# Attention backward loop: keys outermost, one-bank score tiles, own dP tiles, and dQ products in bursts that share a bank with the scores

## The chip, the cores and the metric

The kernel runs on one NeuronCore of a Trainium2 chip. The metric is the device time of one execution in microseconds (us), the median of several runs. All runs quoted here ran on one core, and all are counted as fast: none is more than 1.5% above the fastest run of its kernel. "Granted clock" is the share of its full clock that TensorE was given, as the profile records it.

A *unit* below is 128 queries by 512 keys for a group of four heads. The loop that is changed has 512 units: 8 head groups x 4 query blocks x 4 key blocks x 4 query tiles. A unit takes 20 matmuls, each placed in a quarter of TensorE's array: four scores, four dP, four K products (dK), four V products (dV), four dQ products. Scores and dP contract over 32 rows, so that up to four of them run side by side in different row groups; the others have 16 or 32 output columns and run four side by side in different column groups. I call four such matmuls a *group*.

## The reference, cut to what matters

The reference is a transformer block (layer norm with conditioning, 32-head attention with head size 16, a squared-ReLU MLP; 2048 tokens, width 512) and its gradients for all inputs. The loop in question computes the gradient of this part:

```python
scores = jnp.einsum('bhqd,bhkd->bhqk', q, k) * Dh ** (-0.5)
p = _softmax(scores, axis=-1)
o = jnp.einsum('bhqk,bhkd->bhqd', p, v)
```

For each unit it recomputes E = exp(scores) and forms dP and dS = dP x E. It sums dV from E and dK from dS over the queries. It sums dQ from the transpose of dS over the keys.

## The kernel before

```python
psu = ... tile_pool(name="psIu", bufs=3, space=PSUM)   # three tiles of two banks: scores AND dP
psa = ... tile_pool(name="psIa", bufs=1, space=PSUM)   # accVK and dqacc, a bank each
units = [(hg, qc, kc, qi) for hg in range(HG) for qc in range(QC) for kc in range(QC) for qi in range(4)]

def score_pair(u, pair):                       # two scores, one exp of 128x1024
    psS = psu.tile([P, 2, 512], F32, name="psS_u", tag="pu")
    for hi in range(2):
        r = 32 * (2 * pair + hi)
        PE.matmul(psS[:, hi, :], st["q"][r:r + 32, ...], st["k"][r:r + 32, ...], tile_position=(r, 0), ...)
    ACT.activation(E_u[:, 2 * pair:2 * pair + 2, :], psS[:], AF.Exp, scale=SCALE)

def dp_pair(u, pair):                          # two dP, one multiply of 128x1024
    psD = psu.tile([P, 2, 512], F32, name="psD_u", tag="pu")
    ...
    DVE.tensor_tensor(dS_u[:, 2 * pair:2 * pair + 2, :], psD[:], E_u[...], ALU.mult)

def transpose_unit(u):                         # dS to dS^T by DMA, 512 KB a unit
    SP.dma_start(out=dqt[hg, qc, kc][:, qi], in_=bst[u][1].rearrange("p h k -> p (h k)"), transpose=True)

def kv_quads(u):     # 4 K and 4 V products into accVK; evicted every 4 units, added up by POOL
    ...
def dq_quad(b, kt):  # 4 dQ products into dqacc; evicted every 16 units
    ...

for j in range(2 * NU + 18):                   # two steps a unit
    u = j // 2
    ...
    score_pair(u, j % 2)
    dp_pair((j - 1) // 2, (j - 1) % 2)
    if (j - 1) % 2 == 1: transpose_unit((j - 1) // 2)
    if j % 2 == 0: kv_quads(u - 2)
    v = u - 8
    if j % 2 == 1: dq_quad(block of v, v % 4)  # one dQ group in every unit
```

TensorE, ScalarE and VectorE run this in exactly the written order.

Of the kernel before, what the change touches and what calls it, by code (L numbers as in the profile page):

```python
# [14 lines left out]
AF = mybir.ActivationFunctionType  # L15
ALU = mybir.AluOpType
AX = mybir.AxisListType
BF = dt.bfloat16
F32 = dt.float32

P = 128
# [4 lines left out]
HG = 8  # L26
FF = 1792
FC = 14
SCALE = 0.25
# [5 lines left out]
def kernel(  # L35
# [6 lines left out]
    n = A_x.shape[1]  # L42
    assert A_x.shape[2] == D and n % 512 == 0 and n <= 2048
    TT = n // P
    QC = n // 512
# [7 lines left out]
    PE = nc.tensor  # L53
    DVE = nc.vector
    ACT = nc.scalar
    POOL = nc.gpsimd
    SP = nc.sync
# [50 lines left out]
    dQtP = dram.tile([HG, P, n], BF, name="dQtP")  # L108
    dVKtP = dram.tile([HG, P, n], BF, name="dVKtP")

    with ExitStack() as ph:
        wk = ph.enter_context(tc.tile_pool(name="prepA", bufs=1))
# [20 lines left out]
        for j in range(6):  # L133
            pm = psA.tile([P, 512], F32, name="pm", tag="pm")
            for ic in range(DC):
                PE.matmul(pm[:], sbcT[:, ic, :], wmod_nat[:, ic, j * 512:(j + 1) * 512],
                          start=(ic == 0), stop=(ic == DC - 1))
# [5 lines left out]
        for jb in range(24):  # L143
            for ic in range(DC):
                PE.matmul(pcol[:, jb:jb + 1], wmod_nat[:, ic, jb * P:(jb + 1) * P], siluc_colbf[:, ic:ic + 1],
                          start=(ic == 0), stop=(ic == DC - 1))
# [21 lines left out]
    for ic in range(DC):  # L168
        for t in range(3):
            src = wqkv_nat[:, ic, t * 512:(t + 1) * 512].rearrange("p (hg h d) -> p hg h d", hg=HG, h=4)  # L170
            dst = wpadT[:, ic, t].rearrange("p hg (h c) -> p hg h c", h=4)[:, :, :, 0:DH]
# [524 lines left out]
        POOL.memset(qz[i][:], 0.0)  # L696


    with ExitStack() as ph:
        strm = ph.enter_context(tc.tile_pool(name="phIs", bufs=2))  # L700
        ework = ph.enter_context(tc.tile_pool(name="phIe", bufs=3))
        tpool = ph.enter_context(tc.tile_pool(name="phIt", bufs=3))
        stg = ph.enter_context(tc.tile_pool(name="phIg", bufs=2))
        wk = ph.enter_context(tc.tile_pool(name="phIw", bufs=2))
        psu = ph.enter_context(tc.tile_pool(name="psIu", bufs=3, space=bass.MemoryType.PSUM))
        psa = ph.enter_context(tc.tile_pool(name="psIa", bufs=1, space=bass.MemoryType.PSUM))
        units = [(hg, qc, kc, qi) for hg in range(HG) for qc in range(QC) for kc in range(QC) for qi in range(4)]
        hst, bst, dqt = {}, {}, {}

        def load_head(hg):  # L710
            st = {}
            for key, src in (("q", QtP), ("k", KtP), ("v", VtP), ("do", dOtP)):
                st[key] = strm.tile([P, n], BF, name=f"i{key}", tag=f"i{key}")
                SP.dma_start(out=st[key][:], in_=src[hg])
            st["qz"] = qz[hg % 2]
            qs = strm.tile([P, TT, 64], BF, name="iqs", tag="iqs")
            ACT.dma_start(out=qs[:], in_=q_st[:, :, hg * 64:(hg + 1) * 64])
            POOL.tensor_scalar(qz[hg % 2][:, :, :, DH:2 * DH], qs.rearrange("p t (h d) -> p t h d", h=4),
                               SCALE, None, ALU.mult)
            st["acc"] = stg.tile([P, n], F32, name="dVKacc", tag="dVKacc", bufs=1)  # L720
            st["dq"] = stg.tile([P, n], BF, name="dQst", tag="dQst")
            hst[hg] = st

        def score_pair(u, pair):
            hg, qc, kc, qi = units[u]
            st = hst[hg]
            qt = qc * 4 + qi
            if pair == 0:
                bst[u] = (ework.tile([P, 4, 512], BF, name="E_u", tag="E_u", bufs=4),
                          ework.tile([P, 4, 512], BF, name="dS_u", tag="dS_u", bufs=4))  # L730
            E_u, dS_u = bst[u]
            psS = psu.tile([P, 2, 512], F32, name="psS_u", tag="pu")
            for hi in range(2):
                r = 32 * (2 * pair + hi)
                PE.matmul(psS[:, hi, :], st["q"][r:r + 32, qt * P:(qt + 1) * P], st["k"][r:r + 32, kc * 512:kc * 512 + 512],  # L735
                          start=True, stop=True, tile_position=(r, 0))
            ACT.activation(E_u[:, 2 * pair:2 * pair + 2, :], psS[:], AF.Exp, scale=SCALE)  # L737

        def dp_pair(u, pair):
            hg, qc, kc, qi = units[u]  # L740
            st = hst[hg]
            qt = qc * 4 + qi
            E_u, dS_u = bst[u]
            psD = psu.tile([P, 2, 512], F32, name="psD_u", tag="pu")
            for hi in range(2):
                r = 32 * (2 * pair + hi)
                PE.matmul(psD[:, hi, :], st["do"][r:r + 32, qt * P:(qt + 1) * P], st["v"][r:r + 32, kc * 512:kc * 512 + 512],  # L747
                          start=True, stop=True, tile_position=(r, 0))
            DVE.tensor_tensor(dS_u[:, 2 * pair:2 * pair + 2, :], psD[:], E_u[:, 2 * pair:2 * pair + 2, :], ALU.mult)  # L749

        def transpose_unit(u):
            hg, qc, kc, qi = units[u]
            if qi == 0:
                dqt[hg, qc, kc] = tpool.tile([P, 4, 16, P], BF, name="dsT", tag="dsT")
            SP.dma_start(out=dqt[hg, qc, kc][:, qi],
                         in_=bst[u][1].rearrange("p h k -> p (h k)"), transpose=True)

        cur = {}

        def kv_quads(u):  # L760
            hg, qc, kc, qi = units[u]
            st = hst[hg]
            qt = qc * 4 + qi
            E_u, dS_u = bst.pop(u)
            if qi == 0:
                cur["vk"] = psa.tile([P, 512], F32, name="accVK", tag="accVK")
            acc = cur["vk"]
            for hq in range(4):
                PE.matmul(acc[32 * hq:32 * hq + 32, :], st["qz"][:, qt, hq, :], dS_u[:, hq, :],  # L769
                          start=(qi == 0), stop=False, tile_position=(0, 32 * hq), skip_group_check=True)  # L770
            for hq in range(4):
                PE.matmul(acc[32 * hq:32 * hq + DH, :], dOs_tok[:, qt, (hg * 4 + hq) * DH:(hg * 4 + hq + 1) * DH], E_u[:, hq, :],  # L772
                          start=False, stop=(qi == 3), tile_position=(0, 32 * hq), skip_group_check=True)
            if qi == 3:
                dst = st["acc"][:, kc * 512:(kc + 1) * 512]
                if qc == 0:
                    ACT.activation(dst, acc[:], AF.Identity)
                else:
                    tmp = wk.tile([P, 512], F32, name="vktmp", tag="vktmp")
                    ACT.activation(tmp[:], acc[:], AF.Identity)  # L780
                    POOL.tensor_tensor(dst, dst, tmp[:], ALU.add)  # L781
                if qc == QC - 1 and kc == QC - 1:
                    vkb = stg.tile([P, n], BF, name="vkb", tag="vkb", bufs=1)
                    POOL.tensor_copy(vkb[:], st["acc"][:])
                    SP.dma_start(out=dVKtP[hg], in_=vkb[:])

        def dq_quad(b, kt):
            hg, qc, kc = b
            if kc == 0 and kt == 0:
                cur["dq"] = psa.tile([P, 512], F32, name="dqacc", tag="dqacc")  # L790
            acc = cur["dq"]
            tT = dqt[b]
            for hq in range(4):
                h = hg * 4 + hq
                PE.matmul(acc[32 * hq:32 * hq + 32, :], KS_tok[:, kc * 4 + kt, h * DH:h * DH + 32], tT[:, :, hq * 4 + kt, :],  # L795
                          start=(kc == 0 and kt == 0), stop=(kc == QC - 1 and kt == 3),
                          tile_position=(0, 32 * hq), skip_group_check=True)
            if kt == 3:
                del dqt[b]
                if kc == QC - 1:  # L800
                    ACT.activation(hst[hg]["dq"][:, qc * 512:(qc + 1) * 512], acc[:], AF.Identity)
                    if qc == QC - 1:
                        SP.dma_start(out=dQtP[hg], in_=hst[hg]["dq"][:])

        NU = len(units)
        load_head(0)
        with tc.manual_schedule(engines={PE.engine, ACT.engine, DVE.engine}):
            for j in range(2 * NU + 18):
                u = j // 2
                if j < 2 * NU:  # L810
                    if j % 2 == 0 and units[u][1:] == (0, 2, 0) and units[u][0] + 1 < HG:
                        load_head(units[u][0] + 1)
                    score_pair(u, j % 2)
                if 1 <= j <= 2 * NU:
                    dp_pair((j - 1) // 2, (j - 1) % 2)
                    if (j - 1) % 2 == 1:
                        transpose_unit((j - 1) // 2)
                if j % 2 == 0 and 2 <= u < NU + 2:
                    kv_quads(u - 2)
                v = u - 8  # L820
                if j % 2 == 1 and 0 <= v < NU:
                    hg, qc, kc, qi = units[v]
                    dq_quad((hg, qc, kc), qi)

    qpool.release()

# [202 lines left out]
```

## Time and profile before

| | before |
|---|---|
| time, median | 4181.09 us |
| the loop, first exp to last dQ product | 2214 to 3878 us: 1664 us, 3.25 us a unit |
| in 2300 to 3500 us: TensorE / VectorE / ScalarE busy | 99% / 76% / 68% |
| granted clock there | 0.51 |

Here is the table of windows of the kernel before, for 1200 us inside the loop. Its columns are the stretch, its length, each engine's busy time with the number of instructions, the granted clock, the DMA share and the GB/s.

```profile
core 0: us, PE busy (x) PEld busy (x) DVE busy (x) ACT busy (x) POOL busy (x), PEclk, DMA share, GB/s
2300.00:3500.00 1200.00, 1184.05 (x7420) 207.43 (x7419) 907.53 (x742) 813.84 (x858) 116.39 (x82) 0.51 0.97 180
```

TensorE is without a gap, but at half its clock. VectorE's instructions in the loop are all multiplies, two a unit, so 742 of them are 371 units, or 1200 / 371 = 3.23 us each.

The chain of waits of the kernel before, over one unit (start, length, what):

```profile
2902.89 0.61 PE psD_u L747 x2
2903.50 0.55 PE accVK L769 x4
2904.05 0.43 PE accVK L772 x4
2904.47 0.54 PE psS_u L735 x2
2905.01 0.01 PE psD_u L747 x2
2905.02 0.55 PE dqacc L795 x4
2905.57 0.54 PE psS_u L735 x2
2906.11 0.03 issue
```

These are six phases. In one (at 2904.47) scores and dP run together, and the second costs 0.01 us more. In the other pair they run apart: the scores at 2905.57 (they open the next unit), then the dP at 2906.13, which had to wait for an exp to free one of the three shared tiles.

The clock is 0.50 in almost the whole loop, and 1.00 once, for some 20 us. These are four windows of the kernel before: two ordinary ones, the one just ahead of the rise, and one within the full-clock stretch.

```profile
2500.00:2503.40 3.40, 3.37 (x24) 0.56 (x20) 2.61 (x3) 2.74 (x4) 0.25 (x1) 0.50 0.85 159
2510.00:2513.40 3.40, 3.38 (x22) 0.59 (x23) 2.61 (x3) 2.21 (x3) 0.00 (x0) 0.50 0.82 154
...
3070.40:3073.80 3.40, 3.40 (x26) 0.71 (x24) 2.46 (x3) 2.70 (x4) 0.34 (x1) 0.50 1.38 213
...
3085.00:3090.00 5.00, 4.47 (x42) 1.44 (x40) 4.56 (x4) 4.28 (x5) 0.00 (x0) 1.00 1.49 198
```

TensorE is 99 to 100% busy in the first three.

### The profile page before, as it was taken

What the parts mean: (1) busy time and instruction counts of PE and PEld (TensorE: products, weight loads), DVE (VectorE), ACT (ScalarE), POOL (GpSimd) and SP (SyncE); (2) the same over time, 40 slices, a digit from 0 to 9 for tenths busy, and PEclk for the clock granted to TensorE, in tenths of its full rate; (3) what the DMA queues carried; (4) which work ended last, traced back from release to release, by engine and by line L of the source; (5) the groups of instructions that cost most, each with busy time, mean ns of one, the idle gap of its engine ahead of it and who ended that gap; (6) DMA issues with size and microseconds to landing.
All of it is one profiled execution on the core that took longest, in us unless ns stands there. A gap on an engine that the chain in (4) does not pass through costs nothing.

```text
span 4177.6 us, 48252 instructions
## 1 busy us (share of the span) xinstructions
PE 3479.6 (83%) x18427; PEld 840.9 (20%) x18501; DVE 2070.4 (50%) x3136; ACT 2149.3 (51%) x2462; POOL 294.1 (7%) x314
## 2 busy tenths in 40 slices
PE   3689999999986935766558999999999999999656
PEld 1221111111122311322221111111111111111222
DVE  7640000000038724630056777777777777777582
ACT  0039999999960000000005666666666666666211
POOL 2000000000000000000140000000000000100000
PEclk7975555555557967965875555555555555555777
DMA  3120000000012342466547998999999999999313
GB/s 117 63 111 16 15 6 16 15 16 15 6 65 94 139 110 97 98 210 178 172 151 141 162 195 162 196 163 196 162 200 163 196 163 194 162 172 162 120 48 99
DMA packets 1230133, 497.73 MB, mean 119 GB/s; under 512 B 1162051, under 2 KB 1192263, under 8 KB 1228109
## 3 DMA queue, kind: packets, MB, share of 16 engines
q1 hardware_dynamic: 1207246, 464.23, 50.8%
q0 software_dynamic: 6144, 28.32, 2.3%
q10 hardware_dynamic: 16512, 2.10, 0.4%
q8 instruction: 145, 2.38, 0.2%
q14 instruction: 86, 0.70, 0.1%
HBM read 126.45 MB, written 82.47 MB: 50 GB/s over the span
## 4 chain that ended last, share of the span: by engine, by line
PE 41%; DMA 4%; DVE 3%; issue 3%; ACT 1%; SPq 1%; POOL 0%; ACTq 0%; DVEq 0%; POOLq 0%
PE psS_u L735 13%; PE psD_u L747 7%; PE accVK L769 7%; PE dqacc L795 7%; PE accVK L772 5%; SPq L956 1%; DVE dqkv_tok L860 1%; DMA stld<-stok_st 1%; DVE dh1acc L868 1%; DMA out_dram<-w2blk 0%; ACT E_u L737 0%; DMA iqs<-q_st 0%; POOL dOs_tokpad L620 0%; DMA xst_31079<-dQtP 0%; DMA dsT<-dS_u 0%
## 5 line engine op out<-in xcount | busy, mean ns | idle before, releaser
L749 DVE TENSOR_TENSOR dS_u<-psD_u,E_u 128x1024 bf16<-128x1024 f32 x1024 | 1253.3, 1225 | 451.6 <-PE psD_u L747 384.3
L737 ACT ACTIVATE E_u<-psS_u 128x1024 bf16<-128x1024 f32 x1024 | 1046.8, 1024 | 456.4 <-PE psD_u L747 414.0
L311 ACT ACTIVATE ET<-psST 128x1024 bf16<-128x1024 f32 x1024 | 938.8, 1770 | 0.0
L308 PE MATMUL psST<-qt_sb,kt_sb 32*128 32x512 bf16 x2048 | 622.5, 597 | 79.7 <-DMA kt_sb<-KtP 8.9
L747 PE MATMUL psD_u<-iv,ido 32*128 32x512 bf16 x2048 | 618.1, 594 | 18.6 <-ACT E_u L737 5.3
L735 PE MATMUL psS_u<-ik,iq 32*128 32x512 bf16 x2048 | 615.1, 599 | 12.0 <-DVE dS_u L749 5.4
L326 DVE COPY ostage<-oacc 128x512 f32<-128x512 f32 x32 | 22.1, 692 | 914.4 <-PE oacc L322 799.8
L772 PE MATMUL accVK<-E_u,dOs_tok 128*16 128x512 bf16 x2048 | 329.0, 631 | 0.0
L322 PE MATMUL oacc<-ET,vaug 128*32 128x512 bf16 x2048 | 317.0, 609 | 0.6 <-ACT ET L311 0.6
L795 PE MATMUL dqacc<-dsT,KS_tok 128*32 128x512 bf16 x2048 | 314.1, 604 | 3.3 <-DMA dsT<-dS_u 3.3
L595 ACT ACTIVATE w1blk<-aw_0_12805 128x512 bf16<-128x512 f32 x1 | 0.6, 597 | 554.5 <-PE aw_0_12805 L591 554.5
L735 PEld LDWEIGHTS <-iq 32*128 32x128 bf16 x2048 | 106.7, 99 | 664.8 <-issue 664.5
L308 PEld LDWEIGHTS <-kt_sb 32*128 32x128 bf16 x2048 | 105.4, 99 | 556.7 <-issue 556.7
L781 POOL TENSOR_TENSOR dVKacc<-dVKacc,vktmp 128x512 f32<-128x512 f32 x96 | 121.3, 1264 | 1341.6 <-ACT vktmp L780 1341.6
L747 PEld LDWEIGHTS <-ido 32*128 32x128 bf16 x2048 | 156.4, 100 | 275.2 <-issue 274.4
L769 PE MATMUL accVK<-dS_u,qz_14372 128*32 128x512 bf16 x1024 | 158.8, 608 | 0.0
L769 PE MATMUL accVK<-dS_u,qz_14371 128*32 128x512 bf16 x1024 | 157.0, 602 | 0.0
L515 PE MATMUL pds<-gfT,w2T 128*128 128x512 bf16 x219 | 55.5, 406 | 107.8 <-DVE dzT L518 79.1
L264 PE MATMUL ppad<-xn1T,wpadT 128*128 128x512 bf16 x376 | 96.6, 402 | 21.6 <-DVE stagep L267 16.2
L322 PEld LDWEIGHTS <-vaug 128*32 128x32 bf16 x2048 | 57.7, 102 | 224.1 <-issue 224.1
L795 PEld LDWEIGHTS <-KS_tok 128*32 128x32 bf16 x2048 | 57.8, 101 | 222.3 <-issue 222.0
L328 POOL CAST obf<-ostage 128x512 bf16<-128x512 f32 x32 | 19.6, 614 | 1059.1 <-DVE ostage L326 1059.1
(1251 smaller groups left out, 2776.6 us busy)
## 6 DMA issues: line engine op xcount, KB each, us to landing
dzld<-dztok_st POOLq DMA_DIRECT2D x32, 448.0 KB, 3.7
dzld<-dztok_st SPq DMA_DIRECT2D x32, 448.0 KB, 3.4
dsT<-dS_u SPq DMA_TRANSPOSE x512, 4.3
rT_st<-rT SPq DMA_DIRECT2D x4, 1792.0 KB
rtok_st<-rtok SPq DMA_DIRECT2D x16, 448.0 KB, 2.5
stok_st<-stok SPq DMA_DIRECT2D x16, 448.0 KB
rTb<-rT_st SPq DMA_DIRECT2D x4, 1792.0 KB
rtokb<-rtok_st SPq DMA_DIRECT2D x16, 448.0 KB, 11.7
```

Of the source, the lines that this page charges most:

```text
L264: PE.matmul(pp[:], wpadT[:, ic, which, hg, :], h1T[:, ic, qc * 512:(qc + 1) * 512], start=(ic == 0), stop=(ic == DC - 1))
L308: PE.matmul(ps[:, hi, :], kt_sb[r:r + 32, kt * P:(kt + 1) * P], qt_sb[r:r + 32, qc * 512:(qc + 1) * 512], start=True, stop=True, tile_posi ...
L311: ACT.activation(ET[:, 2 * pair:2 * pair + 2, :], ps[:], AF.Exp, scale=SCALE)
L322: PE.matmul(oacc[32 * hq:32 * hq + 32, :], lhsT, ET[:, hq, :], start=(kt == 0), stop=(kt == TT - 1), tile_position=(0, 32 * hq), skip_grou ...
L735: PE.matmul(psS[:, hi, :], st["q"][r:r + 32, qt * P:(qt + 1) * P], st["k"][r:r + 32, kc * 512:kc * 512 + 512], start=True, stop=True, tile ...
L737: ACT.activation(E_u[:, 2 * pair:2 * pair + 2, :], psS[:], AF.Exp, scale=SCALE)
L747: PE.matmul(psD[:, hi, :], st["do"][r:r + 32, qt * P:(qt + 1) * P], st["v"][r:r + 32, kc * 512:kc * 512 + 512], start=True, stop=True, til ...
L749: DVE.tensor_tensor(dS_u[:, 2 * pair:2 * pair + 2, :], psD[:], E_u[:, 2 * pair:2 * pair + 2, :], ALU.mult)
L769: PE.matmul(acc[32 * hq:32 * hq + 32, :], st["qz"][:, qt, hq, :], dS_u[:, hq, :], start=(qi == 0), stop=False, tile_position=(0, 32 * hq), ...
L772: PE.matmul(acc[32 * hq:32 * hq + DH, :], dOs_tok[:, qt, (hg * 4 + hq) * DH:(hg * 4 + hq + 1) * DH], E_u[:, hq, :], start=False, stop=(qi ...
L781: POOL.tensor_tensor(dst, dst, tmp[:], ALU.add)
L795: PE.matmul(acc[32 * hq:32 * hq + 32, :], KS_tok[:, kc * 4 + kt, h * DH:h * DH + 32], tT[:, :, hq * 4 + kt, :], start=(kc == 0 and kt == 0 ...
```

## The change

Its intent is to give scores and dP PSUM tiles of their own, so that they always overlap. PSUM has eight banks, and before, all were taken. With keys outermost the sum for V and K stays in PSUM for 16 units, and dQ becomes a sum of four groups that is evicted and added up by POOL. So dQ needs its bank only while its four groups run; these are done in a burst in two of every eight steps, and in the other six the bank serves as a third score bank.

```diff
-        psu = ... bufs=3      # 3 x 2 banks, scores and dP
-        psa = ... bufs=1      # accVK, dqacc
-        units = [(hg, qc, kc, qi) for hg ... for qc ... for kc ... for qi in range(4)]
+        psd = ... bufs=2      # 2 x 2 banks, dP
+        pss = ... bufs=2      # 2 x 1 bank, scores
+        psx = ... bufs=1      # accVK; "px": scores or dqacc
+        units = [(hg, kc, qc, qi) for hg ... for kc ... for qc ... for qi in range(4)]
...
+            if shared:
+                psS = psx.tile([P, 512], F32, name="psS_x", tag="px")
+            else:
+                psS = pss.tile([P, 512], F32, name="psS_u", tag="ps")
+            PE.matmul(psS[:], ...)                                       # one score
+            ACT.activation(bst[u][0][:, hq, :], psS[:], AF.Exp, scale=SCALE)   # one exp of 128x512
-            psD = psu.tile([P, 2, 512], F32, name="psD_u", tag="pu")
+            psD = psd.tile([P, 2, 512], F32, name="psD_u", tag="pd")
...  # accVK: evicted once in 16 units, straight to bf16; dqacc: evicted every 4 units, POOL adds
-                if j % 2 == 0 and 2 <= u < NU + 2:
-                    kv_quads(u - 2)
-                v = u - 8
-                if j % 2 == 1 and 0 <= v < NU:
-                    dq_quad((hg, qc, kc), qi)
+                if 2 <= u < NU + 2:
+                    (k_quad if pair == 0 else v_quad)(u - 2)             # K and V in separate steps
+                b = j // 8 - 1
+                if sub >= 6 and 0 <= b < NU // 4:                        # sub = j % 8
+                    for kt in (2 * (sub - 6), 2 * (sub - 6) + 1):
+                        dq_quad(b, kt)
```

(The transposed tiles go from three buffers to two.) The number of matmuls, of evictions (160) and of POOL additions (96) is the same before and after; the exps become 2048 of half the size.

More of the change, by code (lines that the diff above doesn't have):

```diff
@@ L700 @@
         strm = ph.enter_context(tc.tile_pool(name="phIs", bufs=2))
-        ework = ph.enter_context(tc.tile_pool(name="phIe", bufs=3))
-        tpool = ph.enter_context(tc.tile_pool(name="phIt", bufs=3))
+        ework = ph.enter_context(tc.tile_pool(name="phIe", bufs=4))
+        tpool = ph.enter_context(tc.tile_pool(name="phIt", bufs=2))
         stg = ph.enter_context(tc.tile_pool(name="phIg", bufs=2))
         wk = ph.enter_context(tc.tile_pool(name="phIw", bufs=2))
-        psu = ph.enter_context(tc.tile_pool(name="psIu", bufs=3, space=bass.MemoryType.PSUM))
-        psa = ph.enter_context(tc.tile_pool(name="psIa", bufs=1, space=bass.MemoryType.PSUM))
-        units = [(hg, qc, kc, qi) for hg in range(HG) for qc in range(QC) for kc in range(QC) for qi in range(4)]
-        hst, bst, dqt = {}, {}, {}
+        psd = ph.enter_context(tc.tile_pool(name="psId", bufs=2, space=bass.MemoryType.PSUM))
+        pss = ph.enter_context(tc.tile_pool(name="psIs", bufs=2, space=bass.MemoryType.PSUM))
+        psx = ph.enter_context(tc.tile_pool(name="psIx", bufs=1, space=bass.MemoryType.PSUM))
+        units = [(hg, kc, qc, qi) for hg in range(HG) for kc in range(QC) for qc in range(QC) for qi in range(4)]
+        NU = len(units)
+        hst, bst, dqt, cur = {}, {}, {}, {}
         def load_head(hg):
@@ L719, in load_head, with score @@
                                SCALE, None, ALU.mult)
-            st["acc"] = stg.tile([P, n], F32, name="dVKacc", tag="dVKacc", bufs=1)
-            st["dq"] = stg.tile([P, n], BF, name="dQst", tag="dQst")
+            st["acc"] = stg.tile([P, n], F32, name="dQacc", tag="dQacc", bufs=1)
+            st["dq"] = stg.tile([P, n], BF, name="dQst", tag="dQst", bufs=1)
+            st["vk"] = stg.tile([P, n], BF, name="vkb", tag="vkb")
             hst[hg] = st
-        def score_pair(u, pair):
-            hg, qc, kc, qi = units[u]
+        def score(u, hq, shared):
+            hg, kc, qc, qi = units[u]
             st = hst[hg]
             qt = qc * 4 + qi
-            if pair == 0:
-                bst[u] = (ework.tile([P, 4, 512], BF, name="E_u", tag="E_u", bufs=4),
-                          ework.tile([P, 4, 512], BF, name="dS_u", tag="dS_u", bufs=4))
-            E_u, dS_u = bst[u]
-            psS = psu.tile([P, 2, 512], F32, name="psS_u", tag="pu")
-            for hi in range(2):
-                r = 32 * (2 * pair + hi)
-                PE.matmul(psS[:, hi, :], st["q"][r:r + 32, qt * P:(qt + 1) * P], st["k"][r:r + 32, kc * 512:kc * 512 + 512],
-                          start=True, stop=True, tile_position=(r, 0))
-            ACT.activation(E_u[:, 2 * pair:2 * pair + 2, :], psS[:], AF.Exp, scale=SCALE)
+            if hq == 0:
+                bst[u] = (ework.tile([P, 4, 512], BF, name="E_u", tag="E_u"),
+                          ework.tile([P, 4, 512], BF, name="dS_u", tag="dS_u"))
+            r = 32 * hq
+            if shared:
+                psS = psx.tile([P, 512], F32, name="psS_x", tag="px")
+            else:
+                psS = pss.tile([P, 512], F32, name="psS_u", tag="ps")
+            PE.matmul(psS[:], st["q"][r:r + 32, qt * P:(qt + 1) * P], st["k"][r:r + 32, kc * 512:kc * 512 + 512],
+                      start=True, stop=True, tile_position=(r, 0))
+            ACT.activation(bst[u][0][:, hq, :], psS[:], AF.Exp, scale=SCALE)
         def dp_pair(u, pair):
-            hg, qc, kc, qi = units[u]
+            hg, kc, qc, qi = units[u]
             st = hst[hg]
@@ L751, in transpose_unit @@
         def transpose_unit(u):
-            hg, qc, kc, qi = units[u]
+            hg, kc, qc, qi = units[u]
             if qi == 0:
-                dqt[hg, qc, kc] = tpool.tile([P, 4, 16, P], BF, name="dsT", tag="dsT")
-            SP.dma_start(out=dqt[hg, qc, kc][:, qi],
-                         in_=bst[u][1].rearrange("p h k -> p (h k)"), transpose=True)
-        cur = {}
-        def kv_quads(u):
-            hg, qc, kc, qi = units[u]
-            st = hst[hg]
+                dqt[u // 4] = tpool.tile([P, 4, 16, P], BF, name="dsT", tag="dsT")
@@ new lines, in transpose_unit, with k_quad @@
+            SP.dma_start(out=dqt[u // 4][:, qi], in_=bst[u][1].rearrange("p h k -> p (h k)"), transpose=True)
+        def k_quad(u):
+            hg, kc, qc, qi = units[u]
+            qt = qc * 4 + qi
+            if qt == 0:
+                cur["vk"] = psx.tile([P, 512], F32, name="accVK", tag="accVK")
+            for hq in range(4):
+                PE.matmul(cur["vk"][32 * hq:32 * hq + 32, :], hst[hg]["qz"][:, qt, hq, :], bst[u][1][:, hq, :],
+                          start=(qt == 0), stop=False, tile_position=(0, 32 * hq), skip_group_check=True)
@@ L763, in kv_quads, with v_quad @@
+        def v_quad(u):
+            hg, kc, qc, qi = units[u]
             qt = qc * 4 + qi
             E_u, dS_u = bst.pop(u)
-            if qi == 0:
-                cur["vk"] = psa.tile([P, 512], F32, name="accVK", tag="accVK")
             acc = cur["vk"]
             for hq in range(4):
-                PE.matmul(acc[32 * hq:32 * hq + 32, :], st["qz"][:, qt, hq, :], dS_u[:, hq, :],
-                          start=(qi == 0), stop=False, tile_position=(0, 32 * hq), skip_group_check=True)
@@ L771, in kv_quads @@
-            for hq in range(4):
                 PE.matmul(acc[32 * hq:32 * hq + DH, :], dOs_tok[:, qt, (hg * 4 + hq) * DH:(hg * 4 + hq + 1) * DH], E_u[:, hq, :],
-                          start=False, stop=(qi == 3), tile_position=(0, 32 * hq), skip_group_check=True)
-            if qi == 3:
-                dst = st["acc"][:, kc * 512:(kc + 1) * 512]
-                if qc == 0:
-                    ACT.activation(dst, acc[:], AF.Identity)
-                else:
-                    tmp = wk.tile([P, 512], F32, name="vktmp", tag="vktmp")
-                    ACT.activation(tmp[:], acc[:], AF.Identity)
-                    POOL.tensor_tensor(dst, dst, tmp[:], ALU.add)
-                if qc == QC - 1 and kc == QC - 1:
-                    vkb = stg.tile([P, n], BF, name="vkb", tag="vkb", bufs=1)
-                    POOL.tensor_copy(vkb[:], st["acc"][:])
-                    SP.dma_start(out=dVKtP[hg], in_=vkb[:])
+                          start=False, stop=(qt == TT - 1), tile_position=(0, 32 * hq), skip_group_check=True)
@@ L787, in dq_quad @@
+            if qt == TT - 1:
+                ACT.activation(hst[hg]["vk"][:, kc * 512:(kc + 1) * 512], acc[:], AF.Identity)
+                if kc == QC - 1:
+                    SP.dma_start(out=dVKtP[hg], in_=hst[hg]["vk"][:])
         def dq_quad(b, kt):
-            hg, qc, kc = b
-            if kc == 0 and kt == 0:
-                cur["dq"] = psa.tile([P, 512], F32, name="dqacc", tag="dqacc")
+            hg, kc, qc, _ = units[4 * b]
+            if kt == 0:
+                cur["dq"] = psx.tile([P, 512], F32, name="dqacc", tag="px")
@@ L795, in dq_quad @@
                 PE.matmul(acc[32 * hq:32 * hq + 32, :], KS_tok[:, kc * 4 + kt, h * DH:h * DH + 32], tT[:, :, hq * 4 + kt, :],
-                          start=(kc == 0 and kt == 0), stop=(kc == QC - 1 and kt == 3),
-                          tile_position=(0, 32 * hq), skip_group_check=True)
+                          start=(kt == 0), stop=(kt == 3), tile_position=(0, 32 * hq), skip_group_check=True)
             if kt == 3:
                 del dqt[b]
-                if kc == QC - 1:
-                    ACT.activation(hst[hg]["dq"][:, qc * 512:(qc + 1) * 512], acc[:], AF.Identity)
-                    if qc == QC - 1:
-                        SP.dma_start(out=dQtP[hg], in_=hst[hg]["dq"][:])
-        NU = len(units)
+                st = hst[hg]
+                dst = st["acc"][:, qc * 512:(qc + 1) * 512]
+                if kc == 0:
+                    ACT.activation(dst, acc[:], AF.Identity)
+                else:
+                    tmp = wk.tile([P, 512], F32, name="dqtmp", tag="dqtmp")
+                    ACT.activation(tmp[:], acc[:], AF.Identity)
+                    if kc == QC - 1:
+                        dst2 = st["dq"][:, qc * 512:(qc + 1) * 512]
+                    else:
+                        dst2 = dst
+                    POOL.tensor_tensor(dst2, dst, tmp[:], ALU.add)
+                if kc == QC - 1 and qc == QC - 1:
+                    SP.dma_start(out=dQtP[hg], in_=st["dq"][:])
         load_head(0)
         with tc.manual_schedule(engines={PE.engine, ACT.engine, DVE.engine}):
-            for j in range(2 * NU + 18):
-                u = j // 2
+            for j in range(2 * NU + 10):
+                u, pair, sub = j // 2, j % 2, j % 8
                 if j < 2 * NU:
-                    if j % 2 == 0 and units[u][1:] == (0, 2, 0) and units[u][0] + 1 < HG:
+                    if pair == 0 and units[u][1:] == (0, 2, 0) and units[u][0] + 1 < HG:
                         load_head(units[u][0] + 1)
-                    score_pair(u, j % 2)
+                    for hi in range(2):
+                        score(u, 2 * pair + hi, sub < 6 and (2 * sub + hi) % 3 == 2)
                 if 1 <= j <= 2 * NU:
@@ L817 @@
                         transpose_unit((j - 1) // 2)
-                if j % 2 == 0 and 2 <= u < NU + 2:
-                    kv_quads(u - 2)
-                v = u - 8
-                if j % 2 == 1 and 0 <= v < NU:
-                    hg, qc, kc, qi = units[v]
-                    dq_quad((hg, qc, kc), qi)
+                if 2 <= u < NU + 2:
[4 more added lines that the diff above has]
+                        dq_quad(b, kt)
     qpool.release()
```

## The prediction

> **What bounds the kernel now.** The change touches only the backward attention loop. In the timeline its first score matmul starts at 2211 us and its last dQ product ends near 3879 us: 1668 us for 512 units (128 queries by 512 keys), 3.26 us each. The table of windows shows TensorE busy 198 of every 200 us at a granted clock of 0.50, VectorE 151, ScalarE 135. The chain of waits inside the loop is TensorE alone: per unit dP 0.61, K products 0.55, V 0.43, scores with dP 0.54, dQ 0.55, scores 0.54 = 3.22 us. Those are six phases of up to four parallel matmuls where 20 matmuls need five: scores and dP share three PSUM tiles, so every second dP waits for an exp to free its tile and runs alone. The drain at a mode switch (the Trainium skill, "TensorEngine Tiling (Array Packing)", Key Properties) agrees with the trace: a V group following a K group takes 0.43, groups after a switch 0.54-0.55.
>
> **What the change does.** dP gets its own two tiles; scores get one-bank tiles freed by half-size exps. Scores and dP can overlap at every step: 0.54 + 0.55 = 1.09 us a step, two steps a unit. dQ comes in bursts behind a K or V group without a switch, 4 x 0.43 per four units. TensorE at the half clock: (8 x 1.09 + 1.72)/4 = 2.61 us a unit; with two score banks only during the burst, ScalarE starves about 0.75 us twice per four units: about 2.85.
>
> Other floors, per unit. ScalarE: four half exps, about 0.6 each isolated (the 512-wide eviction: 0.598), plus evictions (160 before and after, 0.19): 2.4-2.6. VectorE: 2 x 1.225 = 2.45. Transpose DMAs: at 3074-3094 us, the loop's only stretch at full clock, units ran at 2.37-2.42 us, VectorE without gaps, transposes issued every 2.42 us and then falling behind; about every 20 us an instruction fetch stalls them 1-1.5 us, and head loads use the same queue: I estimate 2.65.
>
> So the new floor is transposes and VectorE, 2.5-2.65, if the clock rises, and TensorE at about 2.85 if it stays at 0.5. The skill ("TensorE: Matmul & The Clock Gate", Part 1) has a half-rate state that sustained activity releases; the 3074 us stretch shows this, after units came closer together. The bursts (16 matmuls in about 1.95 us) should trigger it in much of the loop. A new tight wait: a dQ burst comes 6 steps (7.5 us) after its last transpose's dP, of which VectorE and the landing (4.3-4.5 us) take about 7.
>
> I expect 2.74 us a unit: 512 x 2.74 + 12 = 1415 us, a gain of about 255, all on the critical path. 4181 - 255 = 3926 us; range 3855 to 4035. Faster by over 2%: 0.93; within 2%: 0.05; slower: 0.02.
>
> **What would show it.** Loop of about 1415 us; VectorE near 90% busy in loop windows; dP overlapping scores at nearly every step, TensorE waiting for exps and multiplies instead of gapless; loop clock above 0.6; multiplies waiting for transposes issued 2.4 us apart; POOL additions now for dQ, in the same number; the rest unchanged.
>
> **What would make it wrong.** The clock stays at 0.5 and scores waiting singly for banks break the overlap: three phases a step (1.63 us), and the gain vanishes. Or dQ bursts wait for late transposes, idling TensorE and holding the clock low: above 4035. Or exps run back to back at about 0.5 us and transposes keep up at 2.42: below 3855.

## The result, and the profile after

| | before | after |
|---|---|---|
| time, median | 4183.19 us | 3956.01 us (3950.94 to 3963.36) |
| ratio of the fast runs | | 0.9465 (0.9423 to 0.9507) |
| the loop | 1664 us | 2219 to 3663 us: 1444 us, 2.82 us a unit |
| granted clock, 2300 to 3500 us | 0.51 | 0.85 |

A ratio is the mean time of one kernel's fast runs over that of the other's in the same rounds, so it is not quite the ratio of the medians quoted.

The spans of the two profiled runs differ by 4177.6 - 3961.6 = 216 us, and the loops by 1664 - 1444 = 220 us. Nothing outside the loop moved by more than a few microseconds.

The window of the changed kernel:

```profile
2300.00:3500.00 1200.00, 1027.68 (x8480) 285.11 (x8480) 984.98 (x849) 925.93 (x1829) 120.55 (x88) 0.85 1.15 204
```

TensorE does 14% more matmuls in the same time and is busy for less of it: 86%. VectorE is at 82%, not near the 90% that I predicted. The DMA moves 204 GB/s.

The chain of waits of the changed kernel, over a dQ burst:

```profile
2905.37 4.64 DMA dsT<-dS_u
2910.01 0.14 issue
2910.15 0.61 PE dqacc L792 x8
2910.76 0.32 PE psS_u L740 x2
2911.08 0.01 PE psD_u L752 x2
2911.09 0.32 PE accVK L777 x4
2911.41 0.85 PE dqacc L792 x8
2912.26 0.57 PE psS_u L740 x2
2912.83 0.03 PE psD_u L752 x2
```

Two things are new. Scores and dP overlap (0.01 and 0.03 us for the dP), and their phase takes 0.32 us where the clock is full. And the chain now goes through a transpose, which was nowhere in the chain of a unit before. The waits of the changed kernel, 2300 to 3500 us (who waited for whom: total, times, longest):

```profile
DVE dS_u L754 <- PE psD_u L752: 146.7, 107, 5.2
...
PE dqacc L792 <- DMA dsT<-dS_u: 111.8, 68, 4.3
...
PEld L792 <- DMA dsT<-dS_u: 35.8, 16, 4.6
...
DVE dS_u L754 <- DMA dsT<-dS_u: 21.3, 18, 3.2
...
PE psD_u L752 <- DVE dS_u L754: 15.8, 16, 3.3
```

The clock goes up and down many times. These are four windows of 3.4 us of the changed kernel, each just before a change of the clock:

```profile
2907.80:2911.20 3.40, 1.75 (x22) 0.54 (x25) 2.19 (x2) 1.09 (x3) 0.00 (x0) 1.00 1.13 212
2911.20:2914.60 3.40, 3.40 (x29) 0.72 (x22) 2.83 (x3) 3.20 (x7) 1.27 (x1) 0.51 1.14 210
2917.90:2921.30 3.40, 1.71 (x15) 0.47 (x12) 3.19 (x3) 2.15 (x5) 0.00 (x0) 1.00 1.09 131
2921.50:2924.90 3.40, 3.26 (x28) 0.68 (x28) 1.22 (x1) 1.25 (x3) 0.00 (x0) 0.50 1.20 248
```

After the first and the third, in which TensorE had waited 1.65 and 2.04 us for a transpose, the clock fell to 0.50. After the second and the fourth, with 29 and 28 matmuls at the half clock, it rose to 1.00.

A count that doesn't depend on how a window is laid comes from the traces themselves: in each of the fourteen profiled kernels (those below included) every change of the clock in the loop falls, within a few ns, on a grid of 3.413 us. I count the matmuls in each interval of this grid, each by the share of its time that lies inside (2300 to 3500 us; 2300 to 3300 us for the one kernel whose loop ends earlier):

| in the interval | half clock: clock rises next | full clock: clock falls next |
|---|---|---|
| under 22 matmuls | 0 of 1811 | 344 of 344 |
| 22 to 24 | 37 of 267 | 86 of 194 |
| 24 or more | 395 of 396 | 2 of 1836 |

The kernel before does 20 matmuls in 3.24 us, which is 21.1 in an interval. Of its 344 half-clock intervals, 343 hold fewer than 23, and the one that holds more is the one before its only rise in this stretch. So in these loops, whose matmuls all stream 512 columns through a quarter of the array, the number that TensorE gets through in an interval tells what the clock does next; the share of time for which it is shown as busy does not.

This is as the page says in kind: the Trainium skill, "TensorE: Matmul & The Clock Gate", Part 1, has a half-rate and a full-rate state, set by how busy TensorE was in a window of about 3.4 us.

So the result leaves two questions. Is it the clock that brought the gain, and which part of the change raised it? And what holds the loop at 2.82 us a unit now?

### The profile page after: what moved, and what is told of

Its sections match the earlier page's. It is cut to its first block, busy times and chain, and to the rows that moved or that the text cites. A ratio compares the mean times of both kernels' runs of the same rounds, so it can differ in the third digit from the quotient of the medians.

```text
span 3961.6 us, 49677 instructions
## 1 busy us (share of the span) xinstructions
PE 3084.2 (78%) x18427; PEld 898.6 (23%) x18501; DVE 2005.1 (51%) x3136; ACT 2143.6 (54%) x3486; POOL 279.7 (7%) x306
## 5 line engine op out<-in xcount | busy, mean ns | idle before, releaser
L754 DVE TENSOR_TENSOR dS_u<-psD_u,E_u 128x1024 bf16<-128x1024 f32 x1024 | 1188.5, 1216 | 297.2 <-PE psD_u L752 216.8
L742 ACT ACTIVATE E_u<-psS_u 128x512 bf16<-128x512 f32 x1536 | 868.8, 636 | 290.5 <-PE psD_u L752 276.1
L740 PE MATMUL psS_u<-ik,iq 32*128 32x512 bf16 x1536 | 515.1, 429 | 14.1 <-ACT E_u L742 7.3
L752 PE MATMUL psD_u<-iv,ido 32*128 32x512 bf16 x2048 | 444.3, 428 | 22.5 <-DVE dS_u L754 16.3
L792 PE MATMUL dqacc<-dsT,KS_tok 128*32 128x512 bf16 x2048 | 212.2, 501 | 161.2 <-DMA dsT<-dS_u 133.3
L742 ACT ACTIVATE E_u<-psS_x 128x512 bf16<-128x512 f32 x512 | 334.9, 654 | 3.7 <-PE psD_u L752 1.9
L777 PE MATMUL accVK<-E_u,dOs_tok 128*16 128x512 bf16 x2048 | 225.3, 430 | 0.0
L740 PE MATMUL psS_x<-ik,iq 32*128 32x512 bf16 x512 | 207.5, 405 | 1.0
L807 POOL TENSOR_TENSOR dQacc<-dQacc,dqtmp 128x512 f32<-128x512 f32 x64 | 81.1, 1268 | 849.9 <-ACT dqtmp L802 849.9
L768 PE MATMUL accVK<-dS_u,qz_14371 128*32 128x512 bf16 x1024 | 112.0, 427 | 6.1 <-ACT vkb L780 6.1
L768 PE MATMUL accVK<-dS_u,qz_14372 128*32 128x512 bf16 x1024 | 111.5, 424 | 6.2 <-ACT vkb L780 5.9
```

The source lines that it names most:

```text
L740: PE.matmul(psS[:], st["q"][r:r + 32, qt * P:(qt + 1) * P], st["k"][r:r + 32, kc * 512:kc * 512 + 512], start=True, stop=True, tile_positi ...
L742: ACT.activation(bst[u][0][:, hq, :], psS[:], AF.Exp, scale=SCALE)
L752: PE.matmul(psD[:, hi, :], st["do"][r:r + 32, qt * P:(qt + 1) * P], st["v"][r:r + 32, kc * 512:kc * 512 + 512], start=True, stop=True, til ...
L768: PE.matmul(cur["vk"][32 * hq:32 * hq + 32, :], hst[hg]["qz"][:, qt, hq, :], bst[u][1][:, hq, :], start=(qt == 0), stop=False, tile_positi ...
L777: PE.matmul(acc[32 * hq:32 * hq + DH, :], dOs_tok[:, qt, (hg * 4 + hq) * DH:(hg * 4 + hq + 1) * DH], E_u[:, hq, :], start=False, stop=(qt ...
L792: PE.matmul(acc[32 * hq:32 * hq + 32, :], KS_tok[:, kc * 4 + kt, h * DH:h * DH + 32], tT[:, :, hq * 4 + kt, :], start=(kt == 0), stop=(kt ...
```

## The experiments

All are correct against the reference unless it is said that they are wrong. Loop is from the first exp to the last dQ product of the profiled run, divided by 512 for the unit; the clock is that of 2300 to 3500 us (of 2300 to 3300 us for the changed kernel with half transposes, whose loop ends earlier).

| kernel | median us | ratio to before | unit us | clock |
|---|---|---|---|---|
| before | 4181 to 4187 | | 3.25 | 0.51 |
| changed kernel | 3956.01 | 0.9465 | 2.82 | 0.85 |
| changed kernel again (control) | 3957.35 | 0.9459 | 2.81 | 0.84 |
| loop order alone | 4166.15 | 0.9972 | 3.22 | 0.50 |
| split tiles alone | 4216.51 | 1.0084 | 3.31 | 0.50 |
| dQ bursts alone | 4059.23 | 0.9698 | 2.98 | 0.76 |
| all but the shared bank | 3983.23 | 0.9528 | 2.85 | 0.80 |
| before + 1 group of zeros a unit | 4036.63 | 0.9647 | 3.01 | 0.81 |
| before + 2 groups of zeros a unit | 4034.49 | 0.9643 | 2.96 | 0.98 |
| before, half transposes | 4169.12 | 0.9970 | 3.25 | 0.50 |
| changed, half transposes | 3699.04 | 0.8847 | 2.29 | 0.99 |
| changed, later bursts | 3957.74 | 0.9465 | 2.80 | 0.81 |
| changed, loads from POOL | 3980.75 | 0.9515 | 2.87 | 0.84 |
| changed, both of these | 3991.08 | 0.9532 | 2.86 | 0.79 |

### 1. The loop order alone

```diff
 # in the changed kernel: back to the tiles and the schedule of before
-        psd, pss, psx pools
+        psu (3 x 2 banks, scores and dP), psa (accVK, dqacc)
-  bursts in steps 6 and 7 of 8
+  k_quad, v_quad in even steps; one dQ group in every odd step
+  three transposed tiles, as before
```

> Keys outermost and the swapped accumulations, but the three shared score/dP tiles and the spread dQ groups of before. Theory A (the gain comes from giving scores and dP tiles of their own, which removes the sixth TensorE phase of a unit and lets the clock rise): no gain, 4150 to 4220 us, clock in the loop still 0.50, unit 3.24 us. Rival B (the loop order brings it, through fewer VK evictions and POOL additions): most of the gain, below 4050 us.

It took 4166.15 us, ratio 0.9972 (0.9944 to 1.0), clock 0.50 over 2300 to 3500 us; it had been at 1.00 once, for 51 us near the start of the loop (2251 to 2302 us). The loop order and the swapped accumulations bring next to nothing by themselves. That is theory A's figure; B is out.

### 2. The split tiles alone

```diff
 # in the kernel before
-        psu = ... bufs=3
+        psd = ... bufs=2 (two banks each);  pss = ... bufs=2 (one bank each)
-  one score tile and one exp a pair
+  one score tile and one exp a score
```

> The loop order and spread dQ groups of before, but one-bank score tiles (two banks) and two own dP tiles. Theory A: more than half of the gain of 227 us, so below 4070 us, and a loop clock above 0.6. Rival B: no gain, 4150 us or more. A third theory, C (two score banks are too few without the bank shared with the bursts): ScalarE and TensorE take turns, slower than before or within 2% of it, above 4100 us.

It took 4216.51 us, ratio 1.0084 (1.0065 to 1.0103). My theory A missed: tiles of their own, which were the point of the change in my prediction, made the kernel 0.8% slower. Here is the window of the kernel with split tiles alone, and then two of its waits in the same stretch (who waited for whom: total, times, longest):

```profile
2300.00:3500.00 1200.00, 1152.10 (x7276) 234.93 (x7274) 889.65 (x728) 843.19 (x1568) 114.83 (x82) 0.50 0.95 175
```

```profile
DVE dS_u L750 <- ACT E_u L738: 173.3, 335, 0.9
...
ACT E_u L738 <- PE psS_u L736: 64.2, 343, 0.9
```

ScalarE waits 343 times for a score and VectorE 335 times for an exp; in the kernel before, VectorE waited for an exp once in 2300 to 3860 us. And the clock stays at 0.50, with fewer matmuls in the stretch than before (7276 against 7420). Theory C expected this.

### 3. Everything but the shared bank

```diff
 # in the changed kernel
-                        score(u, 2 * pair + hi, sub < 6 and (2 * sub + hi) % 3 == 2)
+                        score(u, 2 * pair + hi, False)
```

> The changed kernel, loop order and bursts kept, but every score takes one of two banks and the bank that it shared with the dQ bursts is left to dQ alone. Theory S (the third score bank, which the loop order frees between bursts, is what made separate tiles pay): the time goes back to about 4100 to 4230 us, as in the run with tiles alone (4216 us). Rival D (the dense bursts bring the gain, by releasing the clock): below 4020 us with a loop clock above 0.7.

It took 3983.23 us, ratio 0.9528, clock 0.80. The rival D's figure. So C is no answer either: two score banks are enough where the dQ groups come in bursts. The bank shared between scores and bursts is worth 27 us, 0.9528 against 0.9465.

### 4. The bursts alone

```diff
 # in the kernel before, nothing else changed
-                v = u - 8
-                if j % 2 == 1 and 0 <= v < NU:
-                    hg, qc, kc, qi = units[v]
-                    dq_quad((hg, qc, kc), qi)
+                b, sub = j // 8 - 2, j % 8
+                if sub >= 6 and 0 <= b < NU // 4:
+                    for kt in (2 * (sub - 6), 2 * (sub - 6) + 1):
+                        dq_quad(units[4 * b][:3], kt)
```

> The kernel before (its loop order, its three shared tiles), with one thing of the change: the four dQ groups of a block come as two pairs in the last two steps of a block of four units instead of one in every unit, a block later so that none waits for a transpose. Theory H (dense stretches release the clock, and the clock is what the change bought): the clock in the loop rises above 0.65 at least in part of it and the time falls below 4060 us. Rival (the split tiles are needed too): clock 0.50 and 4140 us or more.

It took 4059.23 us, ratio 0.9698 (0.9677 to 0.972), just inside what theory H expected. The same matmuls, the same tiles, the same loop order: only the order of the dQ groups differs. Its window:

```profile
2300.00:3500.00 1200.00, 978.52 (x8066) 225.43 (x8065) 966.30 (x807) 852.81 (x933) 125.08 (x89) 0.76 1.07 194
```

The clock rose from 0.51 to 0.76, and 807 multiplies in place of 742 are 9% more units in the same time. This is 128 us of the 227 us, for four lines. Not all of it need be the clock: at the half clock a burst's two pairs of dQ groups took 0.85 and 0.98 us here, where four groups of the kernel before take 4 x 0.55. That is 0.09 us a unit, by my estimate about 48 us of the loop; the unit fell by 0.27 us.

### 5. and 6. Useless matmuls in the kernel before

If the kernel before is caught at the half clock because its matmuls come too thinly, more matmuls should make it faster. These two kernels multiply dS by zero weights once or twice a unit and add the exact zeros to the K sum:

```diff
 # in kv_quads of the kernel before, behind the four K products
+            for _ in range(1):        # 2 in the second kernel
+                for hq in range(4):
+                    PE.matmul(acc[32 * hq:32 * hq + 32, :], zq[:], dS_u[:, hq, :],
+                              start=False, stop=False, tile_position=(0, 32 * hq), ...)
```

> The kernel before, plus one group of four matmuls a unit with zero weights behind each K group, which adds exact zeros. Theory H (before is caught at the half clock because its units offer too few matmuls per window; a window about 26 matmuls dense released it once): 24 matmuls a unit may be at the edge. If the clock stays at 0.50 the unit grows from 3.24 to 3.67 us and the time to about 4400 us. If it rises above 0.8 the unit is 2.6 to 2.75 us (the 2.37 to 2.45 of the one stretch at full clock plus 0.22) and the time 3860 to 3940 us: more work and yet faster.

> As the run with one group of zero weights, with two. Theory H: the clock rises, the unit is about 2.8 to 2.9 us and the time 3960 to 4020 us, faster than before in spite of 40% more matmuls in the loop. Rival (the clock does not depend on how densely matmuls come): clock 0.50, unit 4.1 us, time about 4620 us.

They took 4036.63 and 4034.49 us, 3.5% and 3.6% less than before. The window of the kernel with two groups of zeros:

```profile
2300.00:3500.00 1200.00, 980.00 (x11400) 299.83 (x11396) 992.06 (x814) 853.04 (x941) 126.39 (x90) 0.98 1.10 197
```

It runs 11400 matmuls where the kernel before runs 7420, and its clock is 0.98. Without a higher clock, two more groups would have made it slower, to about 4620 us as the rival expected. That settles the first question: the kernel before was held by the half clock, and adding matmuls alone was enough to raise it, as the count by intervals has it.

My sizes were off here. With one group the clock is 0.81, as expected, but the time is 97 us above the top of the range, because the clock comes and goes. From 2405 to 3392 us it is at 1.00 seven times, for 10 to 126 us, and between these at 0.50 for 3 to 116 us: 24 matmuls a unit are at the edge. With two groups the time is 14 us above the range.

### 7. and 8. Half of each transpose

Both kernels give a wrong dQ. They transpose only the first two heads of each dS tile, and the dQ products read that half twice:

```diff
-   SP.dma_start(out=dqt[...][:, qi], in_=bst[u][1].rearrange("p h k -> p (h k)"), transpose=True)
+   SP.dma_start(out=dqt[...][:, qi, 0:8], in_=bst[u][1][:, 0:2].rearrange("p h k -> p (h k)"), transpose=True)
-   ... tT[:, :, hq * 4 + kt, :]
+   ... tT[:, :, (hq % 2) * 4 + kt, :]
```

> Wrong result on purpose (dQ): the kernel before with half of each transpose, as was done to the changed kernel, where it took 257 us off. If the transposes became the limit only through the change: no gain, 4150 to 4200 us, unit 3.24 us. If they already held the kernel before: 4100 us or less.

> Wrong result on purpose (dQ): the changed kernel transposes only the first two heads' half of each dS tile, and the dQ products read that half twice. Everything else is as in the changed kernel. If transposes bound its loop (T or L): the loop falls from 1445 us to VectorE's pace of about 2.5 us a unit, so the time falls by 120 us or more, to 3840 us or less. If the half clock or PSUM waits bound it: less than 40 us gained.

Before the change, half the transposes left the time as it was (0.9970, 0.994 to 1.0), and the clock at 0.50. After it, they took 3956 - 3699 = 257 us off. The window of the changed kernel with half transposes:

```profile
2300.00:3300.00 1000.00, 975.00 (x8773) 304.82 (x8771) 992.91 (x878) 946.82 (x1890) 119.33 (x88) 0.99 0.75 138
```

VectorE is busy 992.91 of 1000 us, and the clock is 0.99. So in the changed kernel the transposes are the limit, and behind them VectorE at 2.29 us a unit. They also pull the clock down: waits for them, direct or by way of VectorE, leave TensorE with fewer matmuls in an interval, and with half transposes the clock hardly falls.

### 9. Later dQ bursts

Transposes can hold a loop in two ways: each burst waits for the landing of its last transpose (latency), or the transposes come one after the other at their full rate (throughput). A later burst takes away the first and not the second.

```diff
-            for j in range(2 * NU + 10):
+            for j in range(2 * NU + 18):
-                b = j // 8 - 1
+                b = j // 8 - 2            # and three transposed tiles in place of two
```

> The changed kernel with each dQ burst one block of four units later (three transposed tiles in place of two), so that no burst should wait for its last transpose. Theory L (after the change the loop is held by the latency from dP to the landed transpose, 177 us of TensorE waits on transposes): those waits vanish and the time falls by 80 to 150 us against the changed kernel, to 3810 to 3880 us. Rival T (the transposes are at their throughput, about 204 GB/s of a sustained 215): the waits vanish at TensorE and come back at VectorE, as waits for a free dS tile; the time falls by at most 50 us, 3905 us or more.

It took 3957.74 us, ratio 0.9465, the same as the changed kernel. The waits moved exactly as theory T has it (2300 to 3500 us of this kernel):

```profile
PE psD_u L752 <- DVE dS_u L754: 101.4, 98, 4.4
...
DVE dS_u L754 <- DMA dsT<-dS_u: 94.2, 73, 5.0
```

TensorE's waits for transposes are gone from the list. In their place VectorE waits for transposes to free a dS tile, 94.2 us where it was 21.3, and TensorE for VectorE, 101.4 where it was 15.8. The limit is the throughput. Another reading would be that there are too few dS tiles (four) to cover the latency of a transpose; the trace speaks against it. In this kernel each transpose started on its queue a median 2.8 us after the multiply that completed its dS tile had ended, and none had to wait for a multiply: the queue always had the next one at hand. In the kernel before the same median is 0.03 us.

### 10., 11. and 12. Loads from another queue, and a control

The SP queue issues the transposes and also each head's four loads and two stores. If that queue were the limit, moving the six to POOL should free it:

```diff
-                SP.dma_start(out=st[key][:], in_=src[hg])        # and the stores of dVKtP, dQtP
+                POOL.dma_start(out=st[key][:], in_=src[hg])
```

> The changed kernel with the four loads and two stores of a head issued from POOL instead of SP, whose queue issues the transposes one after the other. If the transposes' queue is the limit, as theory T says, it is freed of about 4 us a head: 15 to 40 us less than the changed kernel, 3915 to 3940 us. If the DMA engines themselves are the limit, the bytes stay and the time with them: within 10 us of the changed kernel.

> Both the later dQ bursts and the loads from POOL. Theory T: the later burst adds nothing of its own (it added 2 us), so within 15 us of the run with the loads from POOL alone.

> The changed kernel unaltered, as a control on the same chip and in the same rounds: 3945 to 3965 us.

The control took 3957.35 us. With the loads from POOL it was 3980.75 us, 0.9515 against 0.9459: slower, which neither of my theories expected. With the later bursts as well it was 3991.08 us, 10 us above the loads from POOL alone, so within the 15 us expected, and the ratios' intervals overlap. The longest single wait in the kernel with loads from POOL shows what went wrong:

```profile
PE dqacc L792 <- DMA dsT<-dS_u: 144.0, 74, 14.5
```

One wait for a transpose now lasts up to 14.5 us, where the longest of the changed kernel was 4.3 us. Three of the moved transfers (iv, ido, dVKtP) took 12.5 to 14.1 us to land. Here the 512 KB transfers from a second queue and the transposes held each other up. It was a queue of another kind, too: the profile lists it as q0, software_dynamic, and the transposes as q1, hardware_dynamic. Whether the limit is the issue of the transposes by their one queue or the DMA engines themselves was not settled: this experiment was to tell and brought a third thing in.

No run beat the changed kernel with a correct result.

## Why the prediction was right or wrong

The time was predicted well: 3926 us with a range of 3855 to 4035, measured 3956. The reason that I put first did not hold, and one that I put second carried it.

- *What bounds the kernel before: TensorE at a clock of 0.50.* Right. More matmuls with a higher clock made it faster (0.9643).
- *"Scores and dP can overlap at every step", from tiles of their own, as the way to a shorter unit.* Wrong as a cause. They do overlap after the change, but split tiles alone gave 1.0084. The step of the prediction that failed is that tiles of their own, by the overlap, shorten the unit: at the half clock, split tiles alone ran at 3.31 us, where the kernel before takes 3.25. I had costed waits for a score bank only during the burst; with two score banks and no bursts, ScalarE and VectorE waited throughout (VectorE 335 times for an exp in 1200 us). The sums at the half clock, 2.61 and "about 2.85" us, had the bursts and the third score bank in them and were never measured: no kernel with bursts stayed at the half clock.
- *"The bursts ... should trigger it in much of the loop."* Right, and this was the main thing: bursts alone gave 0.9698 and a clock of 0.76, more than half of the gain. The full change took the clock to 0.85; I had said above 0.6. The parts do not simply add: loop order alone gave 16 us (its interval of 0.9944 to 1.0 reaches to nothing), split tiles cost 34 us, bursts gave 128 us, and together with the shared bank they gave 227. Bursts, loop order and split tiles gave 203 us (4186 - 3983), and the shared bank the last 27 us (against 3956). With the bursts in place, split tiles and loop order together were worth about 76 us more (4059 - 3983, from different rounds), which neither showed alone; which of the two it is was not separated.
- *"So the new floor is transposes and VectorE, 2.5-2.65".* Right in kind and too low in size, and this is the term of the sum that was mis-sized. The transposes' rate holds the unit at 2.80 to 2.82 us whether the bursts wait for them or not. I had estimated 2.65 from an issue every 2.42 us plus stalls and head loads. Of that difference of about 0.16 us I had allowed 0.09 by saying 2.74 for the whole; the rest is why the loop took 1444 us where I had 1415, and the time 30 us more than predicted. Where the difference between 2.42 and 2.8 us goes can be read from the record of the SP queue, which is never idle for long in the changed kernel (2300 to 3500 us, 424 transposes). Of these, 354 took 2.48 us each; the other 70, during which an instruction fetch started (q8 in the profile, one every 18 us on the average), took 3.60 us, which adds 0.18 us a unit. Issuing the head loads and stores took 31 us, 0.07 a unit, and the short gaps and semaphore steps 41 us, 0.10 a unit: 2.83 us together. That the fetch is the cause of the longer ones is read from their coinciding; no run took it away.
- *VectorE's floor of 2.45.* Too high: in the kernel with half transposes 878 multiplies ran in 1000 us, one every 1.14 us, where the mean duration is 1.21 us: their records overlap. It did not matter, since transposes came first.
- *"A new tight wait: a dQ burst comes 6 steps ... after".* The wait was there (111.8 us of TensorE's, 35.8 of weight loads), but it was no cause. Taking it away moved the same time to VectorE (ratio 0.9465 for both).
- *"VectorE near 90% busy".* It was 82%, which follows from the unit of 2.82 in place of 2.74 and from the shorter multiplies.
- *The rest unchanged, POOL's additions the same in number.* Right (96 both times, and 220 us of the loop against 216 us of the span).

## What to carry to other kernels

A TensorE that the profile shows 99% busy can still be at half its clock, and then the useful question is how many matmuls it gets through in a few microseconds: bunching those of the same kind, without any other change, was worth 3% here, and adding useless ones 3.5%. Test it in minutes by adding matmuls with zero weights: if the time falls, the clock is the limit. When such a limit goes, look at once for what comes next: here the transposes, off the critical path before the change (DMA share 0.97, and 1.15 after it), took over and set the size of the gain; halving one suspect in both kernels showed it in two runs.

## What the Trainium skill lacked or had wrong

- "TensorE: Matmul & The Clock Gate", the closing table under "Why this matters for your kernels", says to keep TensorE busy for at least 4 us continuously to get to the full clock. It lacks that being shown as busy need not be enough: here, with matmuls of a quarter of the array, TensorE was shown busy 1184 of 1200 us at a clock of 0.51. In grid intervals of 3.413 us with fewer than 22 such matmuls of 512 columns the clock never rose (0 of 1811), and with 24 or more it nearly always did (395 of 396).
- The same table says to allow no gaps over about 3 us. Here the clock fell to 0.50 after gaps of 1.65 and 2.04 us, in windows with 22 and 15 matmuls at the full clock.
- "DMA: Bandwidth & Descriptors", section "Latency and other measured facts", gives DMA transposes 261 GB/s, or about 350 to 400 where contiguous. Here transposes of 512 KB within SBUF, when they were the limit, came 424 in 1200 us: 424 x 524288 B / 1200 us = 185 GB/s, and 204 GB/s with the loop's other transfers.
- No page has a figure for what ordinary transfers from a second queue cost a stream of transposes. Moving 512 KB loads and stores to POOL's queue raised the longest wait for a transpose from 4.3 to 14.5 us and the time by 23 us (3980.75 against 3957.35).
- No page says that an instruction fetch goes with a slower transpose. Here a transpose during which one started took 3.60 us on its queue, the others 2.48 us.
